# Attention and two gated MLPs on one core: the last 64 queries of a head pair in two quarters of the array

## The chip, the cores and the metric

The kernel runs on one core of one Trainium2 chip. The metric is the device time of one execution in microseconds (us), the median of several runs. TensorE is called PE, its weight loads PEld, VectorE DVE, ScalarE ACT, GpSimd POOL, and SP is the engine whose queue issues nearly all the transfers.

## The reference

Thresholded attention over 4 batches of 8 heads (576 positions, 64 wide), then two MLPs over the 2,304 tokens:

```python
scores = scale * np.matmul(q, k.transpose(0, 1, 3, 2))
thresh = np.max(scores, axis=-1, keepdims=True) - tau
scores = np.where(scores >= thresh, scores, -1000000000.0)
attn = softmax(scores)                        # with 1e-9 in the divisor
x = np.matmul(attn, v)                        # -> [2304, 512]
h = x @ w_in                                  # [2304, 2048]
g = (a0 + a1*h + a2*h*h + a3*h**3) / (1 + |b0|*|h| + |b1|*h*h + 1e-6)
x = g @ w_out
out = ((x @ w1) * (x @ w2) @ w3) @ w_out2     # [2304, 512]
```

## The kernel before

**Pairs and blocks.** Two heads (64 rows each) share the 128 partitions, so a batch has four pairs `(b, c)`. `load_qk` brings q and k of a pair with the head width on the partitions, into tiles named `raw`; `scale_q` multiplies q by `flag`, which is 0.125 and is worked out from `tau` on the chip. The 576 queries of a pair are five blocks: four of 128 queries (`blk` 0 to 3), and the last 64 queries of both heads together as `blk` 4. `qk` (L496 to L516) multiplies a block with all 576 keys, in two halves of 288 keys, into tiles `S` in PSUM. In float32 each product stands as two records in the trace.

For `blk` 0 to 3 the heads `s` = 0 and 1 take the upper and the lower 64 rows of TensorE's array, and each head writes a PSUM tile of its own (L512). For `blk` 4 there is one product over all 128 rows (L507): its weights are `qp`, a 128x128 tile that is zero but for the two diagonal quarters. `setup` zeroes `qp` once (L402), and `tails` (L490 to L494) copies q's last 64 columns of each head into its quarter, with two POOL copies for each pair. Queries of head 0 thus stand on partitions 0 to 63 of the scores, those of head 1 on 64 to 127.

**After the scores.** `top` takes the maximum (DVE, L521), `thr` the threshold. `exp` has two forms: ACT twice (Prelu L543, Exp L548), or ACT once (Exp L541) and DVE once (L546). Then the weights are normalised, split into two float16 parts and transposed by DMA (`p_t`), and `pv` (L599) multiplies them with v. `pv` uses half of the array's columns for each head, and both heads write the same PSUM tile, on partitions 0 to 63 and 64 to 127.

**The rest of the products.** `mlp1` is `h_product` (L809) and `y_product` (L873), `mlp2` is `ab_product` (L980) and `o_product` (L1009), all of 128x128 weights on 512 columns in float16. The weights come as 72 raw tiles (`raw_w`, L670) that are converted by `conv_w` (L340 or L336, then L681), measured and split (`split_w`, L733 and L734); `w_product` (L930) multiplies w3 with w_out2 in float32.

**Order.** Every step is an event with a number. The table `ORDER` lists the events in the order in which they are issued, with the engine of the steps that may run on several (a is ACT, v is DVE, p is POOL) and the buffers. Each engine runs its instructions in this order; the table was written by a planner that is not part of the kernel.

Of the kernel before, what the change touches and what calls it, by code (L numbers as in the profile page):

```python
# [32 lines left out]
28.0 14.0.1 1 15p 52.1 8.0 0 30v.0 30.0 54v.1 23.0.1 25.0 36.2 27 54.1 29a.0 31.0.2 33.3 31v 33v  # L33
35v 35 48.0 45v.4 50a.0 38p.1 38.2 47 4.1 5.0.0 50.3 9.1 51.0.1 3 10.1 11.0 53.1 55 6.2 7.1 57a.1
44.2 19.5.6 12 32.0 12.0 12 84v.0.0 84 152a.1.1 46a.1 46.4 86.7.8 152 34p.0 34.5 16.2 59.1.3 59a
49.0 21a 37v 39p.0 13v.2.2 13 41v 18v.1 18.6 20.0 17a.3.3 24.1 40.2 43.1 62.1 62a 90.0.1 92.2 64v
64 74a.4 66v 68v.2 94 76 96p.2 78 98.2.1 98a 70p 22v.0 22.7 61.0 100.3 42v.1 100a 102a 102 26p.0
42.8 26.9 72 75.2 119.0.1 56.1 113a.0 80.0.0 17 115 121.3 63a.1 65.1 104a 107v.4 109p 123 63.10
111.2 88v 56 67p.0 77a.1 56 125v.0 127.3.5 127v 129.6 117.0 103.0 129v 67.11 82a 82 77.12 105v.0
105.13 116.1 118a.1 158.0.1 160.0 56 162 131p 131 164a.1 106.2 108p.0 166.4.3 79.0 133v 141v.2 143  # L40
69.0 118.14 154.1.4 120.1 168.0 135a.6 81v.1 168a 81.15 69 166a 137p 69 69 145 139 186.1.0 58a.16
108.17 83.1 83 188.1 132.0 190 192v.2 71v.18 147.0 156a 93.2 195.5.5 170v 197.7 122v.1 122.19 170
180v.8 195a 197a 223.1.0 199a 182 134a.0 199 201v 621.1 203v.2 209v.6 149a 172a 134.20 174v.0
184.1 83 225.2 176p 83 227 229v.0 231.6.3 233.8 89.0 178.0 95p.1 149 85v.21 233a 110.0 231a 110
252.0.1 91a.0 235a 95.22 624v.1 624.23 647.2 171.1 219.0.1 235 205p 91.24 641.0 2 237a 240v.5
246v.4 254.3 256 258p.1 110 650v.1 110 248 260.7.8 211 213 650.25 112a.26 173p.0 97.1 173.27 262.7
114.0 97 262v 124.2 126a.1 97 207 97 645p.0 260v 645.28 221p 290.1.0 163.1 652.0 652 242v 291.0
652 293 99a.29 295a.2 297.0.6 297a 298.3 298a 148.0 165p.0 126.30 140.2 165.31 613.1 150p.1 150.32
314.1.0 142p.0 628.1 630p.1 250.2 264a 155.0 142.33 210.2 300a 300 316.1 613 318 136.1 319a.0 264
274a.2 321.1.4 613 630.34 276 613 321a 179.1 288 302a 304p.1 339.1 278 616v.35 212v.0 284.7.0  # L50
157a.1 212.36 619.0 633.1 633 633 181a.0 218.2 181.37 309a.2 60.0 311 187.1 189p.0 341.2 266v
342a.1 128.0 157.38 268a.3 270v 286v 194.0 633 652 636a.39 130.1 138 220a.1 220.40 655a.41 189.42
215.0 323.8 323a 325p 226.2 217a 234.1 659.0 144.1 146 305v 217 196v.1 196.43 202.0 228v.0 228.44
151.0 153 153 325 159.1 161.0 236p.1 175.0 326v 167.1 169 177 344.2.6 241.2 236.45 243p.0 183.1
185 191.0 193.1 185 244.0 344a 367.0.1 204a.1 312.1 346p 327.1 204.46 198.1 200 365 369.3 272 346
206.0 370 313.0 208 222.1 243.47 372v.2 224.0 230.0 238.1 232 239 214.0 333v.5 335 216 216 245.1
# [36 lines left out]
581v 594p 843.0 561 875.2 908.0 600v.3 851.41 602p 834 846 658.1 660 561 639a 911p.0 854.1 858
935.1 750.0 663a.0 877p.1 935 858 860 860 596.1 750v 665.4.8 620v 665a 580 580 803.0 583 911.11
668.7 806v.9 668a 877.47 526a 671a 604.1 885.1 889p.0 649a.6 651 524 671 776.0 863a.2 526 803v 863
599 889.35 880.0 682a.3 599 601.1.1 601 603a 806.0 812v.52 603 806a 703.1.0 706.2 883.0 812.0
1143.1 685 654.1 606.2 914.1 892.0 894 609.1 708 699.0.6 903.0 906 866v.17 711v.1 611a 916 866 610
713.5.7 687 611 868v.3 812a 605.1 916 868 872v.29 920 1185.3 607a 713a 872 702a 612.2 1166.0 607
920 933 716.1 716a 778a.3.3 642a.3 1166 643p 785.1.0 673a 788.3 646.0 790 925a.41 675v.4 925
793p.2 1171a.0 923v.35 1191.1 778 1191 1196a.1 1194.0 1194 923 615a.0.0 677p 795.7.3 935 1199  # L100
694.1 797.8 797a 795a 1146 928v.47 1199a.0 1152.1 719v 928 1152 615 719 680 1199v 1149.0 1202.2
1149 720v 730a.4 931v.39 1155v.1 1157 737.0.1 723a.2 725p 728.2 1157a.1 740.0 742 1168.0 1207.1
1157v 1160.0 931 733 1207 745a.0 747.0.5 749.7 749a 747a 799v 751a 1213a.1 799 802v 1168 1174
1174v.0 780.1.2 819.1.0 751 754v 756a.0 821.1 1210.1 824 759v 811a.6 762 614.0 1174v 1177.1 814
# [177 lines left out]
def tile_attention_mlps(  # L282
# [16 lines left out]
    nc = tc.nc  # L299
# [326 lines left out]
    def attention(b, c, u):  # L626

        if u:
            at(tails, b, c)
# [610 lines left out]
```

## Time and profile before

| | us |
|---|---|
| median of 3 runs | 1013.68 (1013.58 to 1014.49) |
| the profiled execution | 1015.13 |
| its span, first to last instruction | 1013.3 |
| PE busy in the span | 956.4 |
| DVE, ACT, POOL busy | 788.0, 682.0, 319.7 |

The profiled execution is 1.45 us above the median and 1.8 us above its own span. A busy time is the union of an engine's instructions. The granted clock is a share of PE's full speed, 2.4 GHz; a mean between 0.5 and 1 over a stretch is a mix of the two levels, 1.2 and 2.4 GHz.

### The profile page before, as it was taken

How to read it: one execution, taken by the hardware profiler on the slowest of the kernel's cores; microseconds unless marked ns; L12 is line 12 of the kernel's file. 1: busy time of each engine (PE TensorE's matmuls, PEld its weight loads, DVE VectorE, ACT ScalarE, POOL GpSimd, SP SyncE). 2: the span in 40 equal slices, each digit the busy share in tenths (PEclk: the TensorE clock that was granted, in tenths of full speed). 3: DMA queues.
4: the chain of work that ended last, by engine and by line, in shares of the span. 5: the costliest groups of instructions: out<-in, count | busy, mean ns of one | idle time of the engine just before them, and what ended most of it. 6: DMA issues, size and time to landing. Idle time of an engine off the chain costs nothing.

```text
span 1013.3 us, 15519 instructions
## 1 busy us (share of the span) xinstructions
PE 956.4 (94%) x5260; PEld 460.6 (45%) x5260; DVE 788.0 (78%) x1545; ACT 682.0 (67%) x1274; POOL 319.7 (32%) x347
## 2 busy tenths in 40 slices
PE   2599888899999999999999999999999999999997
PEld 1244443444444545454445454544444444444443
DVE  4886679899988899888878989888887666776831
ACT  3544799999777888887667867886656445554411
POOL 1223134524122434543343443453242212022010
PEclk9999888899999999999999999999999999999999
DMA  6899897988966867996656866975636466333232
GB/s 228 240 254 227 253 246 205 207 217 201 200 133 133 153 153 149 197 180 125 154 118 127 163 148 148 171 145 125 152 71 130 86 112 117 61 70 65 42 83 62
DMA packets 334046, 153.31 MB, mean 151 GB/s; under 512 B 307344, under 2 KB 311440, under 8 KB 333968
## 3 DMA queue, kind: packets, MB, share of 16 engines
q1 hardware_dynamic: 333968, 152.34, 68.3%
q8 instruction: 41, 0.67, 0.3%
q14 instruction: 37, 0.30, 0.1%
HBM read 68.67 MB, written 8.13 MB: 76 GB/s over the span
## 4 chain that ended last, share of the span: by engine, by line
PE 84%; DMA 6%; DVE 4%; ACT 3%; issue 2%; POOL 1%; SPq 0%; ACTq 0%; POOLq 0%; DVEq 0%
PE y L873 17%; PE h L809 17%; PE h L980 12%; PE y L1009 9%; PE S L512 6%; PE S L980 6%; PE h L599 5%; PE h L930 5%; PE y L733 3%; PE S L507 2%; DMA rw<-in_moe_w_out_dram 1%; DMA rw<-in_moe_w_in_dram 1%; DMA x<-gg 1%; DMA pT<-in_v_dram 1%; PE y L734 1%
## 5 line engine op out<-in xcount | busy, mean ns | idle before, releaser
L873 PE MATMUL y<-wp,gt 128*128 128x512 f16 x864 | 201.2, 379 | 0.1
L809 PE MATMUL h<-wp,xp 128*128 128x512 f16 x768 | 178.1, 380 | 0.2 <-ACT r L824 0.2
L980 PE MATMUL h<-wp,yy 128*128 128x512 f16 x576 | 131.8, 379 | 4.6 <-DVE U L831 2.3
L873 PEld LDWEIGHTS <-gt 128*128 128x128 f16 x864 | 82.9, 98 | 104.0 <-issue 6.5
L521 DVE TENSOR_REDUCE m<-S 128x1 f32<-128x576 f32 x144 | 104.2, 749 | 17.7 <-PE S L512 15.9
L809 PEld LDWEIGHTS <-xp 128*128 128x128 f16 x768 | 73.7, 98 | 93.7 <-issue 8.6
L512 PE MATMUL S<-raw 64*128 64x288 f32 x512 | 90.7, 458 | 26.5 <-POOL c L399 10.4
L352 POOL TENSOR_TENSOR gg<-A,r 128x512 f16<-128x512 f32 x38 | 50.7, 1334 | 167.9 <-DVE A L852 112.4
L352 POOL TENSOR_TENSOR hl<-p,hl 128x576 f16<-128x576 f32 x53 | 71.1, 1343 | 93.1 <-ACT hl L336 43.8
L543 ACT ACTIVATE S<-S,th 128x576 f32<-128x576 f32 x119 | 82.5, 708 | 26.6 <-DVE th L359 13.6
L1009 PE MATMUL y<-wp,gt 128*128 128x512 f16 x432 | 99.2, 379 | 0.0
L980 PEld LDWEIGHTS <-yy 128*128 128x128 f16 x624 | 59.8, 98 | 79.6 <-issue 6.3
L817 ACT ACTIVATE U<-h,cf 128x512 f32<-128x512 f32 x72 | 55.8, 776 | 54.1 <-PE h L809 34.3
L548 ACT ACTIVATE p<-S,xy 128x576 f32<-128x576 f32 x119 | 87.9, 741 | 3.5 <-DMA pL<-hl 0.7
L352 POOL TENSOR_TENSOR A<-A,r 128x512 f32<-128x512 f32 x45 | 58.2, 1293 | 90.8 <-ACT r L824 89.3
L512 PEld LDWEIGHTS S<-raw 64*128 64x128 f32 x512 | 49.7, 198 | 65.0 <-issue 18.7
L829 DVE SCALAR_TENSOR_TENSOR U<-h,cf,U 128x512 f32<-128x512 f32 x72 | 53.6, 745 | 27.9 <-ACT U L817 14.3
L839 ACT ACTIVATE r<-A,lnb 128x512 f32<-128x512 f32 x72 | 51.6, 719 | 29.7 <-POOL A L352 18.7
L848 DVE SCALAR_TENSOR_TENSOR gg<-U,cf,r 128x512 f16<-128x512 f32 x72 | 57.8, 804 | 15.3 <-ACT r L841 9.4
L1009 PEld LDWEIGHTS <-gt 128*128 128x128 f16 x432 | 41.6, 98 | 51.8 <-issue 2.7
L681 DVE SCALAR_TENSOR_TENSOR cw<-rw,head 128x512 int32<-128x512 int32 x72 | 52.9, 742 | 11.3 <-POOL head L340 6.6
L821 ACT ACTIVATE A<-h,cf 128x512 f32<-128x512 f32 x72 | 49.1, 683 | 16.4 <-DVE U L831 9.5
(200 smaller groups left out, 1656.3 us busy)
## 6 DMA issues: line engine op xcount, KB each, us to landing
rw<-in_moe_w_dram SPq DMA_DIRECT2D x32, 511.8 KB, 4.4
rw<-in_moe_w_out_dram SPq DMA_DIRECT2D x24, 511.8 KB, 4.3
raw<-in_k_dram SPq DMA_DIRECT2D x32, 288.0 KB, 3.4
rw<-in_moe_w_in_dram SPq DMA_DIRECT2D x16, 511.8 KB, 4.8
wr<-in_v_dram SPq DMA_DIRECT2D x13, 576.0 KB, 4.2
out_dram<-A SPq DMA_DIRECT2D x16, 256.0 KB, 2.5
wr<-in_v_dram SPq DMA_DIRECT2D x12, 320.0 KB, 3.4
d_y<-x SPq DMA_DIRECT2D x13, 256.0 KB, 2.3
```

The costliest lines, as they stand in the source:

```text
L352: (nc.gpsimd if eng[0] == "p" else nc.vector).tensor_tensor(o, x, y, op=op)
L512: nc.tensor.matmul(t[s][:, half, :HS], x[r, o:o + 128], y[r, keys], start=True, stop=True)
L521: nc.vector.tensor_reduce(st["m", b, c, blk][:, s:s + 1], t[:, :, :HS], axis=AX.XY, op=ALU.max, negate=True)
L543: nc.scalar.activation(t, t, AF.Prelu, bias=th, alpha=BIG)
L548: nc.scalar.activation(x, t, AF.Exp, bias=xy[:, 0:1], accum_out=su)
L809: nc.tensor.matmul(t, x[:, y, c, o:o + 128], w[:, a, :], start=c + i == 0, stop=c == KD - 1 and i == 2)
L817: nc.scalar.activation(u, h, AF.Identity, bias=cf[:, 15:16], scale=cf[:, 0:1])
L829: stt(u, h, cf[:, 4:5], u, ALU.mult, ALU.mult)
L848: stt(p[:, 0, :], u, cf[:, 3:4], r, ALU.add, ALU.mult)
L873: nc.tensor.matmul(st["y", n], x[:, 4 * a + j, :], w[:, y, :], start=f + j + i == 0, stop=f == 3 and j == 3 and i == 2)
L980: nc.tensor.matmul(t, x[:, 4 * y + c, :], w[:, a, :], start=c + i == 0, stop=c == KD - 1 and i == 2)
L1009: nc.tensor.matmul(st["o", n], x[:, 4 * a + j, :], w[:, y, :], start=hf + j + i == 0, stop=hf == 1 and j == 3 and i == 2)
```

## The change

`qp`, its zeroing and `tails` go. For `blk` 4 each head's 64 queries are now weights of their own, 64 rows by 64 columns, straight from `raw`: head 0 in the upper left quarter of the array, head 1 in the lower right one. Both write the same PSUM tile as before, each on its own 64 partitions. `ORDER` is a new table: 16 events are gone (the calls of `tails`), and the others stand in a new order with new engines and buffers.

```diff
-28.0 14.0.1 1 15p 52.1 8.0 0 30v.0 30.0 54v.1 23.0.1 25.0 36.2 27 54.1 29a.0 31.0.2 33.3 31v 33v
...
-    qp = cst.tile([128, 128], F32, name="qp")
...
-        nc.gpsimd.memset(qp, 0.0)
...
-    def tails(b, c):
-
-        for s in range(2):
-            r = slice(64 * s, 64 * s + 64)
-            nc.gpsimd.tensor_copy(qp[r, 64 * s:64 * s + 64], st["qk", b, c, 1][0][r, 256:320])
...
-            if blk == 4:
-                nc.tensor.matmul(t[0][:, half, :HS], qp, y[:, keys], start=True, stop=True)
-                continue
             for s in range(2):
                 r = slice(64 * s, 64 * s + 64)
-                o = 128 * (blk % 2)
-                nc.tensor.matmul(t[s][:, half, :HS], x[r, o:o + 128], y[r, keys], start=True,
-                                 stop=True)
+                o = 256 if blk == 4 else 128 * (blk % 2)
+                z, m = (t[0], r) if blk == 4 else (t[s], slice(0, 128))
+                nc.tensor.matmul(z[m, half, :HS], x[r, o:o + (64 if blk == 4 else 128)], y[r, keys],
+                                 start=True, stop=True)
...
-        if u:
-            at(tails, b, c)
```

Lines after the change stand 10 to 14 lower: L512 and L507 become L500, L599 L587, L930 L916, L543 L531, L541 L529, L548 L536.

**PE, the first `blk` 4.** Before, around the zero-padded product of the first pair of batch 0 (the name in front of the arrow is written, those behind are read; xN is N in a row):

```order
L930 MATMUL h<-cw 128x512 x8
L512 MATMUL S<-raw 128x288 x4
L930 MATMUL h<-cw 128x512 x6
L507 MATMUL S<-raw,qp 128x288 x2
L930 MATMUL h<-cw 128x512 x10
L697 LDWEIGHTS onesh
```

Now:

```order
L916 MATMUL h<-cw 128x512 x10
L500 MATMUL S<-raw 128x288 x4
L916 MATMUL h<-cw 128x512 x4
L500 MATMUL S<-raw 64x288 x4
L916 MATMUL h<-cw 128x512 x10
L587 LDWEIGHTS vh
```

Two products became four of half the height at each of the 16 places; what stands around them has hardly moved.

**ACT, the first instructions.** Before (`c_86` takes |tau|, `pa`, `bb` and `c_93` are the coefficients of `powers`, `head` and `rw` belong to `conv_w`, a table load is ACT's own):

```order
L410 ACT_TABLE_LOAD
L410 ACTIVATE c_86<-tau_t 128x1 [waits DMAHW3_49]
L398 ACT_TABLE_LOAD
L357 ACTIVATE th<-m,xy 128x2 [waits DVE_49]
L541 ACTIVATE p<-S,m 128x576 [waits PE_49] x2
L336 ACTIVATE head_102<-rw 128x512 [waits DMAHW7_49,Pool_49]
```

Now:

```order
L417 ACT_TABLE_LOAD
L417 ACTIVATE aa<-pa 128x4 [waits DMAHW1_49]
L418 ACTIVATE bb<-bb 128x2 [waits DMAHW2_49]
L423 ACT_TABLE_LOAD
L423 ACTIVATE c_93<-c_86 128x1 [waits DVE_49]
L424 ACT_TABLE_LOAD
L424 ACTIVATE c_93<-c_93 128x1 [waits Activation_49]
L395 ACT_TABLE_LOAD
L334 ACTIVATE head_101<-rw 128x512 [waits DMAHW3_49,Pool_49]
L406 ACTIVATE c_86<-tau_t 128x1 [waits DMAHW6_49]
```

The coefficients of `powers` moved to the front, with two more table loads, and the first conversion of a weight tile stands ahead of tau.

**DVE, the first instructions.** Before:

```order
L409 TENSOR_SCALAR flag<-tau_t 128x1 [waits DMAHW3_49]
L411 TENSOR_SCALAR xy<-c_86 128x1 [waits Activation_49]
L401 MEMSET xy 128x1
L340 CAST head_102<-rw 128x512 [waits DMAHW0_49,Pool_49]
L681 SCALAR_TENSOR_TENSOR cw<-rw,head_102 128x512 [waits DVE_49]
```

Now:

```order
L425 RECIPROCAL lnb<-c_93 128x1 [waits Activation_49]
L426 SCALAR_TENSOR_TENSOR c_93<-c_86,lnb,c_93 128x1 [waits DVE_49]
L427 TENSOR_SCALAR c_93<-c_93 128x1 [waits DVE_49]
L428 COPY c_93<-pa 128x1
L429 TENSOR_SCALAR c_93<-bb 128x1
L430 MEMSET lnb 128x1
L398 MEMSET xy 128x1
L667 SCALAR_TENSOR_TENSOR cw<-rw,head_101 128x512 [waits DMAHW3_49,Activation_49]
L405 TENSOR_SCALAR flag<-tau_t 128x1 [waits DMAHW6_49]
```

`flag` moved from the first place to the eleventh, behind the part of `conv_w` that waits for ACT's copy.

**ACT, the third and fourth pair of batch 0.** Before, `blk` 1 of the third and `blk` 0 of the fourth pair take ACT's two-step form of `exp`:

```order
L543 ACTIVATE S<-S,th 128x2x288 x2
L548 ACTIVATE p,su<-S,xy 128x576 x2
L357 ACTIVATE su<-su,xy 128x2
L336 ACTIVATE head_102<-rw 128x512
L338 ACTIVATE xp<-h 128x256
L338 ACTIVATE p<-p,su 128x576
L543 ACTIVATE S<-S,th 128x2x288 x2
```

Now both take the one-step form:

```order
L529 ACTIVATE p<-S,m 128x576 x2
L334 ACTIVATE cw<-h 128x512
L336 ACTIVATE xp<-h 128x256
L336 ACTIVATE hl<-p,su 128x576
L677 ACTIVATE sq,acc<-cw 128x512
L334 ACTIVATE head_101<-rw 128x512
L529 ACTIVATE p<-S,m 128x576 x2
```

The second step of these went to DVE. Ahead of ACT's first `y_norm` the two-step form stands 26 times before and 22 times now, the one-step form 10 and 14 times.

## Rows read from the trace of the kernel before

**Rows 1.** The page, its busy times: us, share of the span, instructions.

```profile
PE 956.4 (94%) x5260; PEld 460.6 (45%) x5260; DVE 788.0 (78%) x1545; ACT 682.0 (67%) x1274; POOL 319.7 (32%) x347
```

**Rows 2.** Windows: stretch, length, busy us (instructions), PE clock, DMA share, GB/s.

```profile
0.00:45.00 45.00, 13.40 (x35) 7.25 (x36) 27.48 (x60) 20.31 (x39) 8.33 (x16) 1.00 0.77 232
45.00:115.00 70.00, 69.56 (x236) 31.65 (x236) 49.53 (x90) 35.11 (x71) 19.02 (x22) 1.00 0.92 251
115.00:135.00 20.00, 13.79 (x79) 7.42 (x79) 15.76 (x39) 18.15 (x37) 4.60 (x8) 0.72 1.00 231
158.00:185.00 27.00, 19.34 (x79) 8.54 (x79) 24.98 (x50) 26.84 (x62) 10.45 (x13) 0.75 0.82 196
215.00:960.00 745.00, 739.21 (x4356) 359.66 (x4355) 612.21 (x1186) 523.25 (x957) 251.89 (x259) 1.00 0.65 134
```

**Rows 3.** Timeline of PE, 582 to 587 us: start, length, work.

```profile
583.59 1.13 PE L507 MATMUL S<-raw,qp 128*128 128x288 f32 x4
584.56 2.75 PE L809 MATMUL h<-wp,xp 128*128 128x512 f16 x12
```

**Rows 4.** Windows of line L507 alone: PE, PEld, clock, DMA.

```profile
215.00:960.00 745.00, 15.04 (x52) 9.56 (x52) 1.00 0.65 134
```

**Rows 5.** Timeline of PE, 334 to 352 us.

```profile
336.78 1.17 PE L599 MATMUL h<-pT,vh 128*64 128x256 f16 x18
337.78 0.71 PE L599 MATMUL h<-pT,vl 128*64 128x256 f16 x10
338.43 2.83 PE L873 MATMUL y<-wp,gt 128*128 128x512 f16 x12
341.09 2.75 PE L809 MATMUL h<-wp,xp 128*128 128x512 f16 x12
...
343.68 4.05 PE L873 MATMUL y<-wp,gt 128*128 128x512 f16 x18
347.66 1.24 PE L512 MATMUL S<-raw 64*128 64x288 f32 x8
348.83 1.47 PE L809 MATMUL h<-wp,xp 128*128 128x512 f16 x6
350.14 1.46 PE L873 MATMUL y<-wp,gt 128*128 128x512 f16 x6
```

**Rows 6.** The line of `tails`: its instructions, and who waited for it (us, times).

```profile
L494 POOL COPY qp<-raw x32: 226/234/782, 102.0 to 829.0; 64x64 f32<-64x64 f32 x32
...
POOL hl L340: 6.5, 2
```

**Rows 7.** Timeline of all engines, the first 20 us.

```profile
0.72 1.28 ACT L410 ACT_TABLE_LOAD   x1 [0.72 <-PEq L1227]
...
10.44 2.29 PE L512 MATMUL S<-raw 64*128 64x288 f32 x8 [10.44 <-POOL c L399]
...
16.08 0.78 ACT L336 ACTIVATE head<-rw 128x512 f16<-128x512 bf16 x1 [0.27 <-DMA rw<-in_moe_w_dram]
```

**Rows 8.** The chain that ended last, in its first 60 us: start, length, what.

```profile
2.12 7.06 DMA tau_t<-in_tau_dram
...
16.63 8.04 DMA pT<-in_v_dram
```

**Rows 9.** Groups of the whole span, shapes apart: busy us, mean ns, idle before.

```profile
L548 ACT ACTIVATE p<-S,xy 128x576 f32<-128x576 f32 x119 | 87.9, 741 | 3.5 <-DMA pL<-hl 0.7
L543 ACT ACTIVATE S<-S,th 128x576 f32<-128x576 f32 x119 | 82.5, 708 | 26.6 <-DVE th L359 13.6 <-POOL th L359 10.1 <-PE y L1009 2.4
L548 ACT ACTIVATION_READ_ACCUMULATOR p<-S,xy 128x1 f32 x119 | 23.7, 199 | 0.0
L541 ACT ACTIVATE p<-S,m 128x576 f32<-128x576 f32 x25 | 17.8, 732 | 3.7 <-DVE hl L349 3.5 <-POOL hl L352 0.2
```

**Rows 10.** Timeline of PE and of the SP queue, the last 40 us.

```profile
996.31 11.82 PE L1009 MATMUL y<-wp,gt 128*128 128x512 f16 x54
...
1001.05 1.30 SPq L861 DMA_TRANSPOSE gt<-gg  x1
```

More of the change, by code (lines that the diff above doesn't have):

```diff
@@ L272 @@
[L272 to L277 removed]
+28.0 3 48.1 2 0 50a.0 50.0 14.0.1 1 6.0 36.2 30a.1 30.1 52.1 54a.0 15p 23.0.1 25.0 27 29p.0 31.0.2
@@ new lines @@
+254.3 256 258v.1 260.7.4 260a 73.1 97.0 637.2 262.2 235p 97 173.26 124.0 211 97 97 213 262a 641a.0
+646p.1 288.0.1 646.27 641.28 235 237v 126a.1 99a.29 264p 148.1 150p.0 246a.6 290.0 291 293p.2
+126.30 128.0 264 266a 150.31 163.2 609.1 648.0 140.0 609 248 648 295.0.1 297.5 648 295v 297v
+165a.1 165.32 299a 313.0.1 142v.0 142.33 314.1 316 609 624.1 114.1 626a.1 609 318v.0 274a.7 276
+250.2 626.34 612v.35 179.2 155.0 278 320.1.6 240v.2 242p 320a 337.0 210.1 629.1 181a.0 629 629
+136.1 629 268a.0 270v 157a.1 157.36 299 300a 302p.8 181.37 284.3.4 212p.1 286a 212.38 307a.7 309
@@ new lines @@
+344.1 281.0 486a.0 412 363v.1 524.0 356p.0 303.1 488.7.5 490.6 480 488a 506.0 482p 356.34 686.2
+485 363.4 485 279v 477 310.1 365.1 390p.0 390.7 393.1 469v 487.1 507.0 338.1 428.4 358.1 395
+689p.1 283.1 490a 492a 395.1 283v 395 689.27 509a.1 437.1 487 397v.1 492 524 771.0 423v.39 281a
+416v.36 453.2.8 668a.33 526.1 487 494.1 494 416.1 720.2 674v.21 406a.30 526.1 400a.37 511.0.3
+452.1 526.1 454v 511v 400.0 528 470p.7 402a.31 400a 536.1.0 487p 528 472p 773v.0 496.0 489.2
+438.1.0 416a 411v.32 430.0 432v.41 513v 493a 474.1 429v.26 513 404v.43 402.0 402a 425a.45 697.1
@@ new lines @@
+420a.44 538.1 411.1 429.0 531v 533 496.0 411v 431v 431 429v 539 434a.38 425.1 495p.0 497p 499
+541a.2 543.1.4 672a.46 423.0 773.47 700p.1 496.0 723v.0 708.0 533 545.7 425v 423v 723.6 413a.12
+498 660p.0 498 700.28 545a 433.0 501p 479.0 440.2 535.0 535 503 668.1 435a 432.0 535 535p 668a
+782.1 500v.5 711a.0 542.1 543a 432a 711.23 542 503 409a.25 420.1 561.0.1 427a.4 444.0 442.1 691.1
+420v 406.0 406a 404.1 435 546p 404a 694.0 562.2 759.2 564 566v.0 502 703.1 413.0 455.1 505.1
+785p.1 785.34 505 505 505p 568.2.0 413a 409.0 409v 515v 516p.1 544.1 706 447.1 445.1 544.0 544.1
@@ new lines @@
+1186.1 919 1186 921a.9 639p 1145 786 789v.2 931 642.0 690.1 921 924v.19 1191 1191v.1 671p.1 673p
+924 772.0 791.7.2 791a 793.8 1191v 676 793a 795p 1142.1 1194.2 927v.42 1142 927 774v.0.0 716a
+1148a.1 1150 733.0.1 736.0 719a.1 721p 795 724.2 726a.4 738 1150v.0 1161.1 1066.2 807a.7 810
+741a.1 743.0.3 1150v 1161 1153.0 1167 745.8 1200.0 729 743a 1200 745a 1167a.1 747p 815.0.1 747
+1202.1 1205v.1 750a 752p.5 693a.3.3 817.1 820 755v 821a.0 774 1167v 931 776.1.0 758 1202 778p
+824.1.6 827.3 824a 827a 604 610.0 610 614.0 1208 619 1208p.0 858.0.1 1208p 798a 614.0 860.2 760v.5
@@ new lines @@
+1126a 1131 1126 1353a 1454 1274.1 1332 1613.0 1275.0.0 1309.0 1128.2 1315.0 1277v 1277 1355.7
+1355a 1357p 1357 1334 1274 1315 1134 1235.0 1315 1315p 1359a 1323v 1371.0.1 1276.0 1373.1 1375
+1325a.5 1276.0 1276.0 1327p 1329 1376v.2 1735.0 1378.4.2 1366a.0 1278 1343.1.6 1368 1278 1378a
+1748.0 1735 1360v.3 1235 1253 1253 1739 1380.8 1344p 1380a 1382v 1336.1 1739v.1 1337v 1403.0.1
+1405.2 1255.0 1337 1280p 1255 1317.2 1753.1 1739p 1283 1753 1283 1258.1 1258.1 1258.1 1285.0 1285
+1285 1758a.0 1742.1 1744 1744 1369.1 1382 1262v 1260 1260 1391a.7 1392 1394 1264 1362p 1264 1285v
@@ new lines @@
+1498.0 1517 1498.1 1498.1 1502v 1356 1470p 1500 1519a 1500 1521a.5 1957 1537.1.0 1538.0 1540
+1542v.2 1453.0 1505 1455v 1455 1522p 1961a.1 1473.0 1544.5.7 1506 1477.1 1505 1507.1 1507 1524.2
+1959.0 1545.8 1780a.0 1544a 1507 1545a 1959 1963 1477 1963v.0 1547a 1479.0 1507v 1479.1 1479.0
+1547 1374 1556p.5 1561.1.0 1482 1482 1483.0 1780 1563.3 1484v 1565 1508 1499a.4 1501p 1514.0
+1526.1 1514 1528v.0 1954 1486 1963p 1486 1503 1528 1618.0 1374 1549v 1551v.6 1553v 1533.0.2 1475.0
+1475 1970.1 1558 1535p 1516.1 1516.0 1518 1518 1567a.0 1569.3.4 1570.7 1569a 1970 1516.1 1966.1
@@ new lines @@
+1658 1659p.0 1555 1652.1 1606.0 1626.5.6 1595a 1597v.4 1608v 1599v 1608 1647.0 1557.0 1968 1557
+1982 1982 1573 1575.1 1661.6.7 1601.8 1663.1 1557 1663a 1557v 1559.1 1679.1 1681.3 1683a.1 1661a
+1530 1575 1622.1 1530 1575 1575v 1577.2 1665v 1665 1667v 1684.0.3 1624 1582.1 1684a 1686p 1532.0.0
+1627v 1702.1 1668v.0 1532 1674a.2 1534a 1670p 1986.0 1686 1672 1602.0 1604v 1604 1534 1709.0.1
+1582 1584.1 1711.1 1713 1562.0 1562 1688a 1624.0 1690a.4 1692p 1536.3 1541 1587 1580 1715a.2
+1716.1.8 1584.1 1584.0 1589p 1718.7 1676 1539 1718a 1591 1716a 1720p 1624 2021.4 1587 1782.0
@@ new lines @@
+1974.1.5 1812.0 2233 1847 1976.7 1707.3 1976a 1712 1812 1974a 1812 2241v.0 1946 1992.0.1 1948a
+2243 1900.0 1812v 1847 1930a.4 1849.1 1849 1932 1949a.8 1951v 1849 1901v 1955a.2 1886.1 1901
+1815.1 2243a.0 1886 2243v 2254.0 1956 1888.1 1849v 1888.1 1867.0 1978a 1888.1 1933.0 1867 1978
+1870.0 1870.0 1870.0 1980v 1994.0 1987a.3 1996 1997p.0 2246.0 1999.2.4 2001.6 1890 2001a 1817 1872
+1953 1872 2249 1988 1958 1817 2249 1999a 1890 1960.0 1892p 1895 1895 2003v 1897.0 1897 1897 2003
+1962a 1962 1981v.8 2004v 1983v 2488.1 1874p 1964.2.7 1876 1965a 1851.1 2012v.5 1904.1 2013 1904
@@ L278 @@
+2474 2507a.0 2507p 2508.0 2456v 2457.1 2511 2511 2512a.1 2513 2503 2486 2486 2458 2513v.0 2513v
+2514.2 2487v.1 2509.0 2509 2515 2515 2516a.0 2487 2458 2516 2459v.1 2459
 """
```

436 lines of the change are left out of this document (192 added, 244 removed).

## The prediction

> **What bounds the kernel now.** I read the page's busy times first: PE is busy 956.4 of 1013.3 us [rows 1], so at most 57 us are idle, and every other engine has more room. The windows then show where PE's idle time lies [rows 2]. From 0 to 45 us PE works 13.4 us; from 115 to 135 and from 158 to 185 us it lacks 6.2 and 7.7 us, with the granted clock at a mean of 0.72 and 0.75, so part of both stretches ran at 1.2 GHz. From 215 to 960 us it lacks 5.8 of 745 us at full clock. So the kernel has two regimes: behind 215 us, and from 45 to 115 us (69.56 of 70), PE's own instructions are the time, and a slot of PE that gets longer is paid in full; in the first 45 us and in the two starved stretches the start chain, the loads and ACT (26.84 of 27 us busy) set the end.
>
> **Part one, the products of `blk` 4.** The zero-padded product takes 584.56 - 583.59 = 0.97 us of PE [rows 3]: four records of 288 columns, 0.243 us each, with nothing lost at either side. The new form is not in the trace. Its nearest row is `blk` 0 to 3, two heads in the upper and the lower half of the array, eight records [rows 5]. The pace beside it: 12 full-array products take 343.68 - 341.09 = 2.59 us, 0.216 each. From 343.68 to 350.14 are 6.46 us, and they hold 18 + 6 such products, 5.18 us, and the split block; so that block costs 1.28 us, of which 347.66 to 348.83 is its own slot (1.17) and 0.11 lies ahead of it and behind it. Four rounds of two records side by side explain 0.97; 0.31 is lost in going into the split array and out of it, where the full-array block loses nothing. A quarter block has the same columns and the same two records side by side, so it cannot fall below 0.97; a gain is excluded by that. Its weights are 64 columns wide instead of 128, which may shorten the exposed loads; with the 0.11 at its sides gone it costs 1.17. So the block costs 0.20 to 0.31 us more than before. There are 16: 13 start behind 215 us (52 records in fours [rows 4]), and I count one of the other three as paid in full, since it lies between 45 and 115 us. 14 x 0.265, nearer to the row as it stands, = **+3.7 us**; ends: 13 x 0.20 = 2.6 and 16 x 0.31 = 5.0.
>
> **Part two, `tails` goes.** 32 POOL copies of 234 ns; behind the line POOL's own next cast waited 6.5 us in two places, and PE not at all [rows 6], and POOL is busy 32% [rows 1]. What hides this edit is POOL's idle time; if that cover were gone, 32 x 0.234 = 7.5 us of POOL would be given back, none of it on the path I see. I take **0**. The memset of `qp` is as free.
>
> **Part three, the start.** Before, tau lands at 2.12 + 7.06 = 9.18 [rows 8], and PE starts at 10.44 [rows 7], 1.26 us later, behind `flag` and the scaling of q. Now `pa` and `bb` are loaded ahead, tau is the seventh transfer, and `flag` stands on DVE behind a `conv_w` that waits for ACT's copy, which itself stands behind the coefficients. `bb` is now the third transfer; tau was the fourth, so by its row `bb` is there at about 8.7. Then ACT has three table loads of 1.28 us [rows 7] (a fourth runs while `bb` is on its way), two steps on single columns (taken at 0.2 each, by the accumulator reads [rows 9]) and the copy of 0.78 [rows 7]; then DVE's half of `conv_w`, which has the size of the copy and which I take at 0.78 too, and 1.26 us as before: 8.7 + 3.84 + 0.4 + 0.78 + 0.78 + 1.26 = 15.8; I allow 1.3 less, the length of a load, since `bb` is issued ahead of tau's old place. So PE starts **4.1 to 5.3 us later**. Queued behind this wait are all of DVE and ACT, and the SP queue too, whose next weight load waits for the buffer that DVE's step frees.
>
> But the chain of before does not run through PE's first block alone: it next waits for the last v load, 16.63 to 24.67 [rows 8], whose norm comes after. That load should keep its place. What may come last instead is the second block's chain. I put two blocks at 2 x 2.29 us of PE [rows 7] and, each, two heads by three passes (maximum, exponential, mask) of some 0.73 us [rows 9], 8.8 in sum: 13.4 us in a row, 11 if the second product lies under the first block's passes. From 15.2, the middle, that is 26.2 to 28.6, or 1.5 to 3.9 us behind the v load. From there on both orders have the same steps. I take the lower end, **+1.5 us**, since passes of different engines overlap; ends 0 (the later steps absorb it) and +4 (nearly all of it stays).
>
> By the Trainium skill ("ScalarE: Activation LUTs", What ACT_TABLE_LOAD costs) a load of 1.28 us is followed by a drain of 1.38; the length agrees with [rows 7], the drain no row here shows. By the Trainium skill's figure the three loads would take 4.1 us more, and if all of it stayed the sum would be about 1021.
>
> **Part four, what the new order moves.** Ahead of ACT's first `y_norm` four block halves change their `exp` from the two-step to the one-step form. Each takes 0.708 + 0.741 + 0.199 - 0.732 = 0.92 us from ACT [rows 9], in sum 3.7 us, and gives DVE one pass more. ACT is full in the starved stretch from 158 to 185 us, DVE is at 24.98 of 27 there [rows 2]. So the gain is at most 3.7 us plus what the clock gives back, and it may be a loss where DVE now comes last, as much as 2 us by the room DVE has left there. I take **-1.5 us**. Over the rest of the kernel PE's order is nearly the same sequence of groups, and PE waits for little (5.8 us in 745), so I take 0 there.
>
> **Part five, the tail.** Before, 54 products of 11.7 us stand behind the last products of `ab` and cover its chain, which is down to the last transpose's issue 1001.05 - 996.31 = 4.7 us after they begin [rows 10]. Now 48 products stand there, 10.4 us; a step of the chain moved from POOL to DVE. The cover is shorter by 1.3 us and 5.7 us are left behind the issue for the transpose's 1.30. **0**, within 1 us.
>
> **The sum** is 3.7 + 0 + 1.5 - 1.5 + 0 = +3.7 us on the profiled execution, 1015.13 to 1018.8. That execution is 1.45 us above the median of the runs; the same sum on the median, 1013.68, gives 1017.4, which I round to **1017**.
>
> **The rivals.**
> - *The new order wins.* In the starved stretch from 158 to 185 us ACT's 3.7 us are on the path and go; PE's gaps close and the clock stays up. PE did 19.34 us there at a mean clock of 0.75, which at full clock is 14.5, so up to 4.8 us come back too. With no loss at the start: 3.7 - 3.7 - 4.8 = -4.8, **1009**. It decides from the point where DVE is not late in that stretch. For it: ACT at 99%. Against it: DVE at 93% takes what ACT gives, and the loads (DMA share 0.82) are near.
> - *The order gives back just what the quarters cost*: 3.7 + 0 - 3.7 + 0, within 1 us of before, **1014**.
> - *The start delay stays*: no later step absorbs it, 3.7 + 4 - 0 = +7.7, **1021**.
> - *The quarters do not run side by side*, so the change doesn't do what it says. The two quarters write one PSUM tile, where the halves of L512 write two. Eight records one after the other are 8 x 0.243 + 0.31 = 2.25 us, 1.28 more than now: 14 x 1.28 = 17.9 instead of 3.7, **1032**. Against it speaks `pv`: its 18 + 10 products of 256 columns take 338.43 - 336.78 = 1.65 us [rows 5], while one by one, at half of 0.216, they would take 3.0; and its two heads also write one PSUM tile on different partitions. But those split the array's columns alone. The Trainium skill ("TensorEngine Tiling (Array Packing)", Gotcha 1: PSUM Pressure) says that different row tiles cannot access the same PSUM bank at the same time; the quarters are different row tiles in one bank, so by it this rival would be the result; no row here shows two row tiles in one bank.
>
> **How the numbers follow.** About 0.2%, 2 us, is what a measurement of this kernel can tell from no change: faster is below 1011.7, slower above 1015.7. Chances: the forecast (1015.7 to 1020) 0.35; the start delay stays 0.10; serial quarters 0.08; the order gives back the cost 0.25; the new order wins 0.22. So slower 0.53, same 0.25, faster 0.22. With the ends of the terms together the sum is 2.6 + 0 - 3.7 - 1 = -2.1 to 5.0 + 4 + 2 + 1 = +12, 1011.6 to 1025.7; the first rival lies at 1009. I take 1009 to 1024: it leaves out the serial case, half of what lies beyond 1009 and the sum of all the worst ends. The range of the forecast alone is 1015 to 1021.
>
> **What the profile would show.** The quarter block's slot on PE between two full-array groups: 1.17 to 1.28 us if part one holds, 0.97 if nothing is lost, 2.2 if serial. PE's first record: at 14.5 to 15.8 us instead of 10.44; PE busy in the first 45 us 11 to 13 us instead of 13.4. PE's idle time and clock between 115 and 185 us: 14 us idle and a clock near 0.75 in the same two stretches if the order does nothing there. The tail: PE's last group of L1009 has 48 products and no gap ahead of it. The prediction is wrong if the order changes PE's idle time before 215 us by more than 3 us either way, or if the slot is outside 1.1 to 1.4.

## The result and the profile after

The changed kernel takes 1019.55 us (1018.99 to 1023.85, five runs) against 1014.18 us of before on the same chip. The medians differ by 5.4 us; the ratio on record is 1.0079, interval 1.0063 to 1.0095, which is 6.4 to 9.6 us. Repeated beside the first experiments (run e3_after_again) it was 1020.98 against 1012.38, a ratio of 1.0084 (1.0070 to 1.0099), more than the 4.5 to 6 us expected of the repetition. So the change costs 5 to 10 us. Single runs of it lie up to 5 us apart; the profiled one, 1023.85 with a span of 1022.1, is the longest of the first five, and the second profile has a span of 1016.7. Both are read below, because only what stands in both belongs to the kernel.

The page of the changed kernel, its busy times (compare [rows 1]):

```profile
PE 958.9 (94%) x5324; PEld 454.8 (44%) x5324; DVE 804.2 (79%) x1576; ACT 670.2 (66%) x1232; POOL 318.7 (31%) x327
```

DVE has 16 us more, ACT 12 us less. The windows of the first profile (columns as in [rows 2]):

```profile
0.00:45.00 45.00, 14.54 (x37) 8.06 (x38) 26.58 (x62) 23.86 (x40) 10.52 (x21) 1.00 0.81 240
45.00:115.00 70.00, 69.27 (x268) 32.24 (x268) 47.69 (x90) 38.29 (x72) 17.19 (x23) 1.00 0.91 254
115.00:135.00 20.00, 14.71 (x53) 6.38 (x53) 15.45 (x35) 16.32 (x32) 5.84 (x7) 0.57 0.92 217
158.00:185.00 27.00, 18.93 (x113) 8.36 (x112) 23.82 (x45) 23.50 (x55) 13.14 (x13) 0.81 0.83 205
215.00:960.00 745.00, 734.26 (x4368) 351.86 (x4367) 621.85 (x1208) 508.43 (x925) 244.14 (x238) 1.00 0.65 134
```

The same stretch, 215 to 960 us, in the second profile:

```profile
215.00:960.00 745.00, 734.38 (x4368) 352.64 (x4367) 622.99 (x1207) 505.89 (x919) 241.04 (x236) 1.00 0.65 133
```

And with the quarters under the old order (run e1 below):

```profile
215.00:960.00 745.00, 741.38 (x4408) 355.17 (x4408) 613.43 (x1186) 520.95 (x954) 248.97 (x257) 1.00 0.64 132
```

These rows say the main thing: behind 215 us PE is idle 10.7 and 10.6 us with the new order, in both executions, 5.8 before and 3.6 with the quarters alone. The rest of the difference is found by markers on PE: the fourth `blk` 4 product of the kernel and the last group of `o_product`. In before the fourth block's row (start, length, work) is:

```profile
217.82 1.21 PE L507 MATMUL S<-raw,qp 128*128 128x288 f32 x4
```

Both markers in the first profile of the changed kernel:

```profile
219.41 1.19 PE L500 MATMUL S<-raw 64*64 64x288 f32 x8
...
1007.40 10.52 PE L995 MATMUL y<-wp,gt 128*128 128x512 f16 x48
```

And in the second:

```profile
213.98 1.19 PE L500 MATMUL S<-raw 64*64 64x288 f32 x8
...
1002.00 10.52 PE L995 MATMUL y<-wp,gt 128*128 128x512 f16 x48
```

PE's last group ends at 1017.92 and 1012.52, at 1008.13 before [rows 10]. The account, in us against the profile of before:

| | first profile | second profile |
|---|---|---|
| up to the fourth `blk` 4 | +1.6 | -3.8 |
| PE's idle time behind it (wait by wait: 10.7 and 10.6, 5.6 before) | +5.1 | +5.0 |
| the quarters behind it, by run e1 | +2.1 | +2.1 |
| PE's other work behind it | +1.0 | +1.1 |
| from PE's end to the end (4.2, before 5.2) | -1.0 | -1.0 |
| sum: 1022.1 and 1016.7 against 1013.3 | +8.8 | +3.4 |

Line four is what is left of PE's own time when the others are taken off, and its cause stays open. It is not other work: behind the fourth block the traces of both kernels hold the same number of products of each kind (696 of `h<-wp,xp`, 576 of `h<-wp,yy`, and so on).

The first line says little. One execution of a kernel differs from the next by as much: the fourth block starts at 217.82, 216.54, 215.59 and 214.95 us in four traces of the old order (before, and the runs e4, b1 and e1 below, whose edits hardly touch this stretch), at 219.41, 213.98 and 214.05 in three of the new one (two profiles of the changed kernel, and run g1). The two groups overlap, so an effect of the new order up to there can't be told from zero. Behind the block the two profiles agree: +7.2 us in both.

Who PE waited for between 215 and 960 us in the second profile (us, times, longest):

```profile
PE h L587 <- DVE U L817: 1.8, 2, 1.3
PE h L966 <- DVE xp L347: 1.3, 1, 1.3
PE h L966 <- DVE fw L939: 1.3, 1, 1.3
PE y L995 <- DMA gt<-gg: 1.0, 1, 1.0
PE S L966 <- DMA x<-gg: 0.8, 1, 0.8
```

There are 18 waits of at most 1.3 us, most of them on DVE, DMA and ACT (16 in the first profile); before has 7. Most stand at the same places in both profiles (327 and 322 us for the first row, 841 and 836 for the fourth), so they are the order's and not chance.

### The profile page after: what moved, and what is told of

It is laid out like the page before. It is cut to its first block, busy times and chain, and to the rows that moved or that the text cites. A ratio compares the mean times of both kernels' runs of the same rounds, so it can differ in the third digit from the quotient of the medians.

```text
span 1022.1 us, 15648 instructions
## 1 busy us (share of the span) xinstructions
PE 958.9 (94%) x5324; PEld 454.8 (44%) x5324; DVE 804.2 (79%) x1576; ACT 670.2 (66%) x1232; POOL 318.7 (31%) x327
## 4 chain that ended last, share of the span: by engine, by line
PE 47%; DVE 3%; DMA 2%; ACT 2%; issue 1%; POOL 0%; SPq 0%; ACTq 0%; DVEq 0%; POOLq 0%
PE y L859 11%; PE h L795 10%; PE h L966 7%; PE y L995 6%; PE S L966 6%; PE S L500 4%; PE h L587 2%; DMA gt<-gg 1%; DMA raw<-in_k_dram 1%; DVE m L509 1%; DMA pT<-hl 0%; DVE hl L347 0%; DMA x<-gg 0%; DVE U L817 0%; DVE U L815 0%
## 5 line engine op out<-in xcount | busy, mean ns | idle before, releaser
L500 PE MATMUL S<-raw 64*128 64x288 f32 (+1 forms) x640 | 107.8, 445 | 34.2 <-ACT p L536 15.6
L531 ACT ACTIVATE S<-S,th 128x576 f32<-128x576 f32 x112 | 78.0, 710 | 33.0 <-DVE th L357 13.5
L350 POOL TENSOR_TENSOR A<-A,r 128x512 f32<-128x512 f32 x50 | 67.5, 1351 | 88.2 <-ACT r L810 87.4
L500 PEld LDWEIGHTS S<-raw 64*128 64x128 f32 (+1 forms) x640 | 57.0, 183 | 80.9 <-issue 26.4
L536 ACT ACTIVATE p<-S,xy 128x576 f32<-128x576 f32 x112 | 82.7, 740 | 4.9 <-DMA pT<-hl 1.4
L350 POOL TENSOR_TENSOR hl<-p,hl 128x576 f16<-128x576 f32 x49 | 65.5, 1337 | 60.7 <-ACT hl L334 30.5
L834 DVE SCALAR_TENSOR_TENSOR gg<-U,cf,r 128x512 f16<-128x512 f32 x72 | 55.7, 774 | 17.9 <-ACT r L827 11.9
L667 DVE SCALAR_TENSOR_TENSOR cw<-rw,head 128x512 int32<-128x512 int32 x72 | 55.5, 777 | 11.0 <-POOL head L338 6.3
L916 PE MATMUL h<-cw 128*128 128x512 f32 x128 | 58.3, 609 | 0.0
```

What stands on the lines that cost most here:

```text
L350: (nc.gpsimd if eng[0] == "p" else nc.vector).tensor_tensor(o, x, y, op=op)
L500: nc.tensor.matmul(z[m, half, :HS], x[r, o:o + (64 if blk == 4 else 128)], y[r, keys], start=True, stop=True)
L531: nc.scalar.activation(t, t, AF.Prelu, bias=th, alpha=BIG)
L536: nc.scalar.activation(x, t, AF.Exp, bias=xy[:, 0:1], accum_out=su)
L834: stt(p[:, 0, :], u, cf[:, 3:4], r, ALU.add, ALU.mult)
L916: nc.tensor.matmul(t, st["cw", ("w3", m, j // 4)][:, o:o + 128], st["cw", ("wo2", j)], start=j == 0, stop=j == 7)
```

## The experiments

Each run is compared with runs of the kernel before beside it, whose median was 1012.38 in the first four, 1011.93 in the next four and 1012.60 in the last three.

**The quarters alone.** In the kernel before:

```diff
-                nc.tensor.matmul(t[0][:, half, :HS], qp, y[:, keys], start=True, stop=True)
+                for s in range(2):
+                    r = slice(64 * s, 64 * s + 64)
+                    nc.tensor.matmul(t[0][r, half, :HS], qp[r, 64 * s:64 * s + 64], y[r, keys],
+                                     start=True, stop=True)
```

> The kernel before with its own order and its copies of tails; only the product of blk 4 is changed: each head's diagonal quarter of qp is a weight tile of 64 x 64, so PE does the four quarter products. Theory A (the quarters cost about what the forecast said, the new order costs the rest by more waits of PE behind 215 us): 2.6 to 4 us above before, slot of a quarter block 1.1 to 1.3 us. Theory B (the quarters cost all of the 5.4 us, by losses next to their slots): 5 us or more above before. Theory C (the quarters cost nothing, the order all): within 1 us of before, slot 0.97 us.

1013.75 us, ratio 1.0018 (1.0004 to 1.0031): 0.4 to 3.1 us above before. PE's timeline around a quarter block, start and length (the answer to [rows 3]):

```profile
771.93 1.19 PE L509 MATMUL S<-raw,qp 64*64 64x288 f32 x8
773.05 1.47 PE L812 MATMUL h<-wp,xp 128*128 128x512 f16 x6
```

The slot is 1.12 us, against 0.97; in the changed kernel it is 1.11 or 1.12 in 15 of 16 blocks. Where a block stands between full-array products, the stretch from it to the next one is 0.25 us longer than before (114.48 against 114.23, 33.56 against 33.31, 28.22 against 27.97): 0.15 in the slot, 0.10 beside it. But from the fourth block to the last, 12 blocks on, PE's time without its waits grew by 2.0 us only (692.60 - 3.59 against 692.59 - 5.56), 0.17 a block; at four blocks of before the padded slot was 1.04 or 1.05 and not 0.97. Theories B and C fall; A holds, with a smaller price than it named. But for the copies of `tails`, whose cost can't be told from zero (run e4 below), this run and the changed kernel differ by `ORDER` alone: 1.0018 against 1.0084 puts 6.7 us on the new order.

**Each quarter twice.** The loop of run e1 goes over the two heads twice.

```diff
-                for s in range(2):
+                for s in range(4):
+                    s %= 2
```

> The quarters in the old order (run e1) with each quarter product issued twice into the same place, so that a block has 16 records in the divided array instead of 8. If a block's cost is four rounds of two records side by side and a fixed loss at the change of the array's division: slot 1.12 + 0.97 = 2.1 us, 16 x 0.97 = 15.5 us above e1. If the loss belongs to each product (loads that are not hidden): slot 2.2 to 2.4 us. If quarters of one PSUM tile did not run side by side: 1.9 us more a block.

1026.57 us, 1.0134 (1.0119 to 1.0149). The slot:

```profile
783.64 2.16 PE L510 MATMUL S<-raw,qp 64*64 64x288 f32 x16
785.73 1.47 PE L813 MATMUL h<-wp,xp 128*128 128x512 f16 x6
```

2.09 us, 0.97 more for eight more records: in pairs they cost 0.243 each, as the padded records do. So the quarters run side by side in one PSUM tile, their own pace is the full one, and the loss is a fixed one for each block (0.15 in the slot with 8 records as with 16); that it arises at the change of the array's division is the reading that fits.

On the clock the run is 11.7 us above e1 by the ratios, and not 15.5. From the fourth block to PE's end it took 802.35 us against 790.47, so the 13 blocks there make 11.9 of it. What the three blocks ahead of 215 us cost is too small for the clock, whose intervals are 1.5 us either way, to tell.

**`tails` alone, and the padded product in the new order.** The first (e4) leaves the body of `tails` out:

```diff
     def tails(b, c):
-        for s in range(2):
-            r = slice(64 * s, 64 * s + 64)
-            nc.gpsimd.tensor_copy(qp[r, 64 * s:64 * s + 64], st["qk", b, c, 1][0][r, 256:320])
+        return
```

> The kernel before without the 32 POOL copies of tails: qp stays zero, so the scores of the last 64 queries are zero. The price of part two of the forecast alone. If the copies are hidden: within 0.5 us of before. If POOL's copies hold up what PE waits for: 1 us or more below before.

1011.84 us, 0.9995 (0.9985 to 1.0005): no change that can be told from zero, as forecast.

The second (e2) puts `qp`, its copies and the padded product back into the changed kernel:

```diff
+            if blk == 4:
+                nc.tensor.matmul(t[0][:, half, :HS], qp, y[:, keys], start=True, stop=True)
+                continue
...
     def scale_q(b, c, u):
         x = st["qk", b, c, u][0]
         copy(x, x, flag)
+        if u:
+            st.setdefault("ahead", []).append((b, c))
+            tails()
```

> The changed kernel with its new order, but with the old zero-padded product for blk 4; the two POOL copies for qp stand behind the scaling of q's second part, or behind the product of the pair before where that comes later. Theory A: 1.5 to 3 us above before, since the new order's waits stay. Theory B: within 1 us of before. Theory C: about 5 us above before.

1024.36 us, 1.0119 (1.0102 to 1.0136), 12 us above before: none of the three theories named that. It is 3 us above the changed kernel although 15 of the 16 slots are back at about 1.0 us. PE's idle time between 215 and 960 us is 12.3 us. The copies stand where the table was not made for them, so this run doesn't price the order alone, and what of the 3 us is theirs stays open. Without its waits PE takes 2.9 us longer behind the fourth block than in before although the quarters are gone, so lines three and four of the account above can't be separated by this run either.

**Engines or sequence.** Run f1 gives every step of the changed kernel the engine that it had before; f2 gives run e1 the new engines; f3 sets back only the second step of `exp`. Three of the lines, with names for numbers and v for DVE, a for ACT (f1 has all such lines, f3 those of exp, f2 the reverse):

```diff
-exp(0,2,1,0) v
+exp(0,2,1,0) a
-p_norm(0,0,1) a
+p_norm(0,0,1) v
-p_norm(0,1,0) v
+p_norm(0,1,0) a
```

> The changed kernel with its new sequence and buffers, but every step on the engine that it had in the kernel before (550 steps differ). The first runs put about 7 us on the new order. Theory E (the engines: DVE, with 16 us more work, comes late for PE behind 215 us): about 3.5 us above before, PE idle 4 to 6 us between 215 and 960 us. Theory S (the sequence and the buffers): 7 to 9 us above before, idle 9 to 12 us. Theory J (a sequence fits only the engines that it was made for): more than 9 us above before.

> The kernel of the quarters in the old sequence (run e1), with the engines of the changed kernel. Theory E: 7 to 9 us above before. Theory S: 1 to 4 us above before, as e1. Theory J: more than 9 us above before.

> The changed kernel with the second step of exp on the engine of before in all blocks (33 steps differ, 7 more on ACT than in the changed kernel); all else as in the changed kernel. If the moved exponentials make DVE late: 2 us or more below the changed kernel, so 5 to 6 us above before. If they don't matter behind 215 us: within 1 us of the changed kernel. By the forecast's part four (ACT is the late engine from 158 to 185 us) it is 1.5 us above the changed kernel.

1129.03 us (1.1160), 1091.14 us (1.0782) and 1035.70 us (1.0225, 1.0207 to 1.0244). Theory J holds beyond what it named: with f1, PE has 59 waits behind 215 us, 73 us in sum. Either sequence with the other's engines loses some ten times as much as the two kernels differ by, and even the 33 exponentials make the changed kernel 14 to 15 us slower, which none of the three expectations of f3 named. With these runs the 7 us of the new order can't be divided into a part of the engines and a part of the sequence.

**Single waits.** Run g1 moves six steps of the changed kernel, b1 two steps of before. The edits in the tables, with the event's name in place of its number, g1 first and b1 second:

```diff
-scale_q(1,0,1)
 act_h(2,3)
...
 num(2,3)
+scale_q(1,0,1)
...
+num(9,0)
+num(9,0)
 c_mul(7,1)
...
-num(9,0)
-num(9,0)
...
-quotient(10,0)
 pv(3,0,0)
+x_split(3,0,0)
+x_split(3,0,0)
+quotient(10,0)
 top(3,1,1,1)
...
-x_split(3,0,0)
...
-x_split(3,0,0)
```

```diff
-p_lo(1,0,2,1)
 act_h(4,0)
 act_h(4,0)
 num(3,3)
 num(3,3)
+p_lo(1,0,2,1)
...
 num(8,3)
+num(8,3)
 p_t(2,2,3,0)
...
 quotient(8,2)
-num(8,3)
```

> The changed kernel with six of its steps moved by at most 13 places in the order, at three of PE's waits for DVE behind 215 us (1.33, 0.49 and 1.29 us in the second profile of the changed kernel): scale_q(1,0,1) goes behind num(2,3), num(9,0) ahead of the c_mul of group 7, and x_split(3,0,0) directly behind its pv. Theory W (behind 215 us PE is the bound and each of its waits is paid in full): the three waits go, and the time falls by 2 to 3.1 us against the changed kernel, to 4 to 6.5 us above before. Rival (the waits are slack that turns up elsewhere): idle between 215 and 960 us stays at 10 to 11 us, and the time within 0.7 us of the changed kernel.

1020.40 us, 1.0072 (1.0056 to 1.0089). DVE at the first place, in the second profile of the changed kernel:

```profile
317.41 1.40 DVE L340 TENSOR_SCALAR raw<-raw,flag 128x320 f32<-128x320 f32 x1
...
320.76 0.75 DVE L817 SCALAR_TENSOR_TENSOR U<-U,cf,h 128x512 f32<-128x512 f32 x1
```

PE there:

```profile
321.56 1.17 PE L587 MATMUL h<-pT,vh 128*64 128x256 f16 x18 [1.33 <-DVE U L817]
```

And in run g1:

```profile
320.69 1.17 PE L587 MATMUL h<-pT,vh 128*64 128x256 f16 x18 [0.32 <-DVE U L817]
```

With the scaling of q out of the way the wait fell from 1.33 to 0.32, and the stretch from the fourth to the fifth quarter block from 151.79 to 150.50 us: paid in full, and not taken back there. At the second place the wait of 0.49 us at 649 us went, and one of 0.32 came at 647. At the third place the wait of 1.29 us (0.39 in the first profile) went, and two new ones came within 9 us:

```profile
668.47 1.17 PE L587 MATMUL h<-pT,vh 128*64 128x256 f16 x18 [0.73 <-ACT r L810]
...
677.16 2.53 PE L795 MATMUL h<-wp,xp 128*128 128x512 f16 x11 [1.68 <-ACT U L336]
```

That stretch, between the twelfth and the thirteenth quarter block, became 0.98 us longer. So idle between 215 and 960 us fell from 10.6 to 10.0 us only, and the gain on the clock, about 1 us, is inside the intervals. Theory W fails as a forecast of the time, and the rival is right on idle. Both places say the same of the mechanism: a wait counts in full, but where several engines are close behind, taking one away can make the next.

> The kernel before with two of its steps moved by at most 11 places, at its two waits of PE for DVE behind 215 us (0.97 at 363 us and 1.36 at 623 us): p_lo(1,0,2,1) goes behind num(3,3), and the second half of num(8,3) directly behind the first. Theory W: 1.5 to 2.3 us below before. Rival: the same as before.

1010.99 us, 0.9984 (0.9971 to 0.9998): 0.2 to 2.9 us below before. PE's waits from 215 to 960 us, complete but for two of 0.2 us:

```profile
PE h L980 <- DMA yy<-d_y: 1.0, 1, 1.0
PE h L599 <- DVE xp L349: 0.6, 1, 0.6
PE S L507 <- issue: 0.4, 1, 0.4
PE h L980 <- DVE acc L701: 0.4, 1, 0.4
PE h L980 <- ACT U L338: 0.3, 1, 0.3
```

The 0.97 us are gone, of the 1.36 us 0.32 are left. The wait for `yy` fell too, from 1.9 to 1.0 us; no edit touches it, and it is 1.0 in run e4 and 1.1 in e1 as well, so it is the execution's. The ratio is the lowest of the study, but not clear of that of run s1 below.

**The start.** One step of before is moved:

```diff
 raw_w(wo2,3)
+powers
 load_qk(0,0,0)
 limits
...
 qk(0,0,1)
-powers
```

> The kernel before with one step moved: powers (two transfers, four steps of ACT, eight of DVE) is the second event instead of the 34th, so tau is the sixth transfer and flag stands behind the coefficients. PE's first product comes 1 to 3 us later than 10.4 us. By the forecast's part three about a third of the delay stays: 0.5 to 1.5 us above before. If the delay is hidden behind the v load, as the start of the changed kernel suggests: within 0.5 us of before, and PE's first product of L930 at the same time as before.

1011.36 us, 0.9992 (0.9982 to 1.0001). The expected delay did not come at all: PE's first product starts at 10.48 us, since `bb` landed at about 5.3 and the coefficients were done when tau came, at 9.24. `powers` in front does not by itself delay the start. In the changed kernel the copy and `conv_w` stand ahead of `flag` as well, so there the coefficients and their table loads hold it up (rows in the next section).

The second thing expected, PE's first L930 at the time of before, was missed: it came 2.9 us earlier than the 44.59 of before.

```profile
41.66 3.39 PE L930 MATMUL h<-cw 128*128 128x512 f32 x4
```

With `pa` and `bb` no longer between them, the two last v loads were issued from 15.27 on, and from 16.16 in before.

## Why the prediction came out right, and where it did not

Forecast were 1017 us, slower, within 1009 to 1024; measured 1019.55. The direction and the range held, but that the sum came near is luck: three terms were off, two of them (+1.5 and -1.5) cancelled, and the largest part of the result was taken at 0. The prediction's own signs of being wrong did not come: the slot is 1.12, and PE is idle 48.3 and 46.2 us ahead of 215 us, against 45.9 before. Two of its other signs were missed: PE's first record came ahead of the 14.5 to 15.8 named, and in the first 45 us PE was busy for 14.54 and 15.80 us instead of 11 to 13.

**The regimes** hold. Behind 215 us a wait of PE is on the path (run b1, and the first place of run g1), and the time up to 215 us varies between executions by more than the change moves it: the fourth block comes at 219.41 and 213.98 us in two executions of the changed kernel.

**Part one** named the right mechanism. The slot of 1.12 us and the 0.25 us of a block that stands alone lie within 0.20 to 0.31. The term was mis-sized: 14 x 0.265 = 3.7 took every block at the price of a lone one, and run e1 gives 2.0 us for 12 blocks, 0.4 to 3.1 us in all on the clock. The lower end, 2.6, lies above the 2.1 that this price makes for 13. At the price of the lone block 13 would make 3.2. Part of the gap is "with nothing lost at either side", read from one padded block: four of the 13 behind 215 us took 1.04 or 1.05, 0.3 us in sum; where the rest went was not traced. The serial rival (2.25 us a block) is out by the slot itself and by run d1. The Trainium skill says in "TensorEngine Tiling (Array Packing)", Gotcha 1: PSUM Pressure, that different row tiles cannot access the same PSUM bank at the same time; the slot of 1.12 us, for two quarters on different partitions, does not agree. Another place of the Trainium skill, "PSUM — Partial Sum Buffer", PSUM bank collisions raise a hardware error, says that different quadrants (blocks of 32 partitions) of a bank don't collide, which it measured between engines; the slot agrees.

**Part two**, 0, is right (run e4).

**Part three** had the wrong sign. PE's first product came 3.2 us later, at 13.63 instead of the forecast 14.5 to 15.8, because `bb` landed at 6.0 and not at the 8.7 taken from tau's row. A place in the queue does not tell the landing: tau was used at 9.20 as the fourth transfer (before), at 9.24 as the sixth (run s1) and at 7.40 as the fourth again (run b1). The changed kernel from `bb` on: ACT's chain up to the copy, then DVE's `flag` and its second step of `conv_w`, and the v loads behind that step:

```profile
6.01 0.20 ACT L418 ACTIVATE bb<-bb 128x2 f32<-128x2 f32 x1 [1.16 <-DMA bb<-in_moe_b_dram]
6.24 1.28 ACT L423 ACT_TABLE_LOAD   x1
7.53 0.20 ACT L423 ACTIVATE c<-c 128x1 f32<-128x1 f32 x1
7.75 1.28 ACT L424 ACT_TABLE_LOAD   x1
9.04 0.20 ACT L424 ACTIVATE c<-c 128x1 f32<-128x1 f32 x1
...
10.56 0.77 ACT L334 ACTIVATE head<-rw 128x512 f16<-128x512 bf16 x1
...
11.97 0.15 DVE L405 TENSOR_SCALAR flag<-tau_t 128x1 f32<-128x1 f32 x1
...
12.10 0.68 DVE L667 SCALAR_TENSOR_TENSOR cw<-rw,head 128x512 int32<-128x512 int32 x1
...
13.18 0.90 SPq L457 DMA_DIRECT2D pT<-in_v_dram  x2
13.63 2.29 PE L500 MATMUL S<-raw 64*128 64x288 f32 x8 [13.63 <-POOL raw L340]
```

The same step of DVE and the same two loads in before:

```profile
14.13 0.68 DVE L681 SCALAR_TENSOR_TENSOR cw<-rw,head 128x512 int32<-128x512 int32 x1
...
16.16 0.91 SPq L461 DMA_DIRECT2D pT<-in_v_dram  x2
```

The step that failed is "That load should keep its place". The queue waits for that step of DVE before it issues the late v loads: the first of them went out at 14.84 in before and at 12.81 now, 0.03 us behind the step's end. In before the step stood behind the first block's maximum, and `pa` and `bb` were issued between it and the last two loads; now neither is so, and those two go out from 13.18 on instead of 16.16. ACT squares the last of v at 21.33, in before at 24.69, when it had landed. So PE's steady work began earlier in spite of the later first product, at 42.87 instead of 44.59 us, and at 41.61 in the second profile. PE's first L930 in before:

```profile
44.59 2.08 PE L930 MATMUL h<-cw 128*128 128x512 f32 x2
```

The same product in the first profile of the changed kernel:

```profile
42.87 3.60 PE L916 MATMUL h<-cw 128*128 128x512 f32 x5
```

And in the second:

```profile
41.61 4.53 PE L916 MATMUL h<-cw 128*128 128x512 f32 x8
```

At this point that is -1.7 to -3.0 us instead of +1.5, against one profile of before (44.16 in run e1, 44.59 in e4, 42.51 in b1, where tau came early). That the v load is what moved it was not tested alone; run s1, with earlier v loads and an unmoved first product, points the same way. By the fourth block nothing of it is left that the traces can tell. The mechanism of the start delay's rival is out, though its number, 1021, lies nearer to the measured times than the forecast's 1017.

**Part four** expected ACT's relief to reach PE, and it did not. From 158 to 185 us ACT fell from 26.84 to 23.50 us in the first profile and to 25.50 in the second; but it is 25.32 there in run e1 too, with the old order, so this window does not show how much of the 3.7 came. PE lacks 8.1 and 8.2 us there instead of 7.7. PE's waits in that stretch of before:

```profile
PE S L507 <- issue: 2.6, 1, 2.6
PE y L733 <- ACT wp L336: 2.5, 2, 1.9
PE S L512 <- ACT p L548: 1.6, 2, 1.0
PE h L713 <- DVE xl L349: 1.0, 1, 1.0
```

In the first profile of the changed kernel:

```profile
PE h L587 <- DVE xp L347: 3.3, 1, 3.3
PE S L500 <- ACT p L536: 2.9, 1, 2.9
PE y L720 <- DVE wp L340: 1.3, 1, 1.3
```

And in the second:

```profile
PE S L500 <- ACT p L536: 4.0, 2, 2.9
PE h L699 <- DVE wsc L696: 1.9, 1, 1.9
PE h L587 <- DVE xp L347: 1.7, 1, 1.7
```

DVE, which the text had named as the point from which the first rival decides, is now late for 3.6 to 5.0 us in sum (1.0 before), and ACT still for 2.9 to 4.5 (4.1 before): what one engine was relieved of the other took. The -1.5 us were not there. The worse miss is the clause after it: "Over the rest of the kernel PE's order is nearly the same sequence of groups, and PE waits for little (5.8 us in 745), so I take 0 there." PE's own sequence hardly moved, but DVE had about 10 us more behind 215 us and 550 steps had another engine, and PE's waits grew by 5 us. That is the largest term of the result, and it was taken at nothing. Likeness on PE's queue says little about waits; the queues of those that PE waits for have to be compared.

**Part five** holds: no wait stands ahead of the last group, its 48 products cover the chain, and the end fell by 1.0 us, at the edge of the 1 us allowed.

Together, 3.7 + 1.5 - 1.5 + 0 stood for about 2 (the quarters), nothing that can be told from zero (all up to 215 us), +5 (waits behind it), +1 (open) and -1 (the end): 7 us, between the 5.4 and the 8.6 by which the two pairs of medians differ.

## What to carry to other kernels

Where one engine is the bound, price the waits of that engine as carefully as its work: a new order that leaves its queue alike can still add ten waits of 0.5 us, and where one was taken out and no new one came, the time came back in full. A block in a divided array between full-array products costs a fixed 0.17 to 0.25 us here, the same in its slot with 8 and with 16 records, so it is counted by places and by what stands beside them. One profile of each kernel is too little for a stretch that differs by 3 to 5 us from one execution to the next. And an order with its assignment of engines is one thing: half of it taken from another table cost 79 and 117 us.

## What the hardware showed

- Two quarters of one PSUM tile, on different rows and columns of the array, run side by side: 16 records take 0.97 us more than 8.
- Behind a table load of 1.28 us the next ACT instruction starts at once (6.24 + 1.28 = 7.52, start at 7.53). The drain of 1.38 us that the Trainium skill gives ("ScalarE: Activation LUTs", What ACT_TABLE_LOAD costs) is not seen in these rows, nor the 4.1 us for three loads.
- Single DVE steps took more than twice their usual time while a POOL step ran beside them: in the second profile L836, two inputs in SBUF, took 1.78 us (mean of its 72 in the first profile 0.732) at 671.64, 0.05 us behind a POOL step of 1.28 us. The Trainium skill ("GPSIMD Engine Reference", Specifications) names contention for DVE steps with two inputs in SBUF, or in a 2-port mode; the scaling of q at 317.41, with one tensor input, took 1.40 us against 0.38 in four of its six, and a POOL step of 1.66 us had begun at 316.96. Whether it ran in such a mode no row shows, and that contention is the cause was not tested.
